# Five edits around the last weights and the stores of an attention and soft-MoE kernel

## The chip, the core and the metric

The kernel runs on one core of a Trainium2 chip. The metric is device time in microseconds (us) of one execution. Five engines work from queues of their own: TensorE (PE in the profile; PEld is its weight load), VectorE (DVE), ScalarE (ACT), GpSimd (POOL) and SyncE (SP). Data moves between the chip's DRAM and the on-chip memory by 16 DMA engines, which the profile shows as a mean busy share and as GB/s. GB/s counts the bytes that are written, so a load of float32 that is cast to bfloat16 on its way shows half of what it reads.

## The reference, cut to what matters

```
scores = q @ k^T / 8, masked                 # q, k, v: (4, 8, 768, 64) float32
a = softmax(scores);  attn = a @ v           # heads 0, 2, 6 causal; the others: 4 first keys + window of 64
x = attn as (3072, 512)
logits = x @ phi                             # phi: (512, 32)
slot_input = softmax(logits, over the 3072 rows)^T @ x       # (32, 512), 4 slots for each of 8 experts
slot_out[e] = relu(slot_input[e] @ w1[e]) @ w2[e]            # w1: (8, 512, 1024), w2: (8, 1024, 512)
out = softmax(logits, over the 32 slots) @ slot_out          # (3072, 512) float32
```

q, k and v are 6.3 MB each, w1 and w2 16.8 MB each, phi 64 KB, and the output is 6.3 MB.

## The kernel before

The program writes down every piece of work as an operation with its engines, an estimated duration, a key, the operations it depends on and the buffers it takes. A small list scheduler in the kernel (`Plan.run`) then places them in order of time, and the instructions are emitted in that order; each engine runs its own list strictly in order. So the keys and estimates decide the order, and the chip's time is what comes of it.

**Loads.** All of q, k, v and the weights but half of w1[0] are loaded by GpSimd (`dma`, L343 to L351), one queue, in a fixed order, cast to bfloat16 on the way. The order ends with the w2 matrices; the last two, 14 and 15 in the code's count (experts 6 and 7 of w2), are loaded in column halves of 256 (`load_half`, L395): left half of 14, left half of 15, right half of 14, right half of 15 (L976 to L979). SP issues three loads at the start (`sp_front`, L480): half of w1[0], the flags, and phi, in this order. phi is cast by DVE (L548), transposed twice by PE and copied to its place (L534 to L555); later products of x and phi read it.

**Attention** runs batch by batch, two heads at a time: scores on PE (L665), exponentials on ACT (L735), masks on DVE (L681), products with v on PE (L809), normalisation on DVE (L833), transposes, and the sums for the slots.

**The experts** follow once all rows are there: products with w1 (L1017), relu (L1027), transposes, and products with w2 (`w2_op`, L1050 to L1066), which add all experts into one bank. Experts 0 to 5 are done for all 512 columns, then experts 6 and 7 for the left 256 columns, and later for the right 256. While PE waits for the last weight of a half, `wait_zeros` (L1070) has it multiply zeros: three such products of 448 columns before the last product of the left half (ZT0), two before that of the right half (ZT1).

**The output.** The sums of a half are scaled into `slot_out` by one instruction (`emit_so`, L1110 to L1115; the scheduler gives both to ACT). Then each block of 128 rows takes one product on PE (L1130) and one scaled copy from the bank on DVE (L1140) or ACT (L1138) into a staging buffer. The first 12 blocks, three groups of four, are done in column halves: all left halves once the left half of `slot_out` is there, all right halves once the right half is there. The other 12 blocks are done for all 512 columns at the end. A group of four blocks is 512 rows of the output, and partition p holds rows 4p to 4p+3.

**The stores** (`store`, L1146). Left halves of group 0: two stores by GpSimd, of one and of three blocks. Left halves of groups 1 and 2: two stores each by SP, of two blocks. Right halves: two stores for each group by SP. The last three groups: one store of 1 MB each by SP.

Of the kernel before, what the change touches and what calls it, by code (L numbers as in the profile page):

```python
# [14 lines left out]
ACT = mybir.ActivationFunctionType  # L15
# [211 lines left out]
def kernel(  # L227
# [13 lines left out]
    nc = tc.nc  # L241
# [5 lines left out]
    NE, DM, F = moe_w1.shape  # L247
# [6 lines left out]
    banks = []  # L254
# [20 lines left out]
    phf = sb.tile([P, 4 * NS], F32, name="phf")  # L275
# [33 lines left out]
    def tr_bf(s, n):  # L309
# [6 lines left out]
    slot_out = mk[:, 640:1152]  # L316
# [4 lines left out]
    pl = Plan({"S8": 11, "QT": 2, "KT": 2, "VT": 1, "VB": 2, "VF": 3, "PT": 2, "PTX": 2, "XB": 2,  # L321
               "XT": 1, "SC": 2, "TR": 2, "PV": 1, "BK": 8})
# [6 lines left out]
    def on(eng, occ, late=0.18):  # L329
        return {eng: (occ, occ + late)}  # L330
# [12 lines left out]
    def dma(name, nbytes, buf, dst, src, deps=()):  # L343
        if len(chain) >= 8:
            deps = list(deps) + [chain[-8]]
        iss = pl.op("issue " + name, on("POOL", 0.645, 1.4), -100, deps=list(deps) + [fifo[0]],
                    acq=[buf] if buf else [], lead=1.3, emit=lambda o: nc.gpsimd.dma_start(dst(), src))  # L347
        fifo[0] = iss
        took = nbytes / (395000.0 if nbytes == 1 << 20 and name != "w0" else 423000.0)
        chain.append(pl.op("land " + name, {"DMA": (took, took + 1.85 + 0.05 * len(chain))}, -100, deps=[iss] + chain[-1:], lead=5.2))  # L350
        return chain[-1]  # L351

# [23 lines left out]
    NW, NSPLIT = 2 * NE, 2  # L376
    wbuf = [Buf("S8") for _ in range(NW)]
    wland = [None] * NW
# [11 lines left out]
    def w_half(i, c):  # L390
        return late_mem[i]()[:, 2048 * c:2048 * (c + 1)].rearrange("p (a f) -> p a f", a=8)

    hland = {}

    def load_half(i, c, deps=()):  # L395
        src = moe_w2[i - NE].rearrange("(fi fo) d -> fi fo d", fo=8)[:, :, 256 * c:256 * (c + 1)]
        hland[i, c] = dma(f"w{i}.{c}", 1 << 20, None, lambda: w_half(i, c), src, deps=deps)

    def load_w(i, deps=()):
        if i == 0:  # L400
# [79 lines left out]
    def sp_front(o):  # L480
        nc.sync.dma_start(w0f, moe_w1[0].rearrange("(di h x) f -> h di (x f)", h=2, x=2)[0])
        nc.sync.dma_start(ri, ri_src)
        nc.sync.dma_start(phf, moe_phi.rearrange("(p a) s -> p (a s)", a=4))

    load_part("q", 0, 0)
    load_part("k", 0, 0)
# [202 lines left out]
    for b in range(B):  # L689
        for n in range(4):  # L690
            p = 4 * b + n
# [55 lines left out]
        for ns in ([(0, 1), (2, 3)] if b == 0 else [(0, 1, 2, 3)]):  # L747
# [18 lines left out]
            def emit_mx(o, b=b, ns=ns):  # L766
# [5 lines left out]
                      emit=emit_mx)  # L772
# [274 lines left out]
    so = Buf("BK")  # L1047
    w2o = {}

    def w2_op(e, c0, c1):  # L1050
        def emit_w2(o):
            e4, g0 = e // 4, e % 4
            for fo in range(8):
                g = fo % 4
                nc.tensor.matmul(banks[so.slot][32 * g:32 * (g + 1), 256 * c0:256 * c1],
                                 hT_t[e4][:, fo, 32 * g0:32 * (g0 + 1)], w_row(NE + e, fo) if c1 - c0 == 2 else w_half(NE + e, c0)[:, fo, :],
                                 start=(e == 0 and fo < 4), stop=(e == NE - 1 and fo >= 4),
                                 tile_position=(0, 32 * g), skip_group_check=True)

        land = [wland[NE + e]] if c1 - c0 == 2 else [hland[NE + e, c0]]  # L1060
        o = pl.op(f"W2.{e}" + ("" if c1 - c0 == 2 else f".{c0}"), on("PE", 0.22 * (c1 - c0), 0.27),
                  kt + (29 + e if c0 == 1 else 16 + e),
                  deps=[hte[e // 4]] + land + [w2o[c] for c in range(c0, c1) if c in w2o],
                  acq=[so] if e == 0 else [], emit=emit_w2, mode="c32", mm=8)
        for c in range(c0, c1):
            w2o[c] = o  # L1066

# [2 lines left out]
    def wait_zeros(name, n, key, dep, first=False):  # L1070
        def emit_z(o):
            for _ in range(n):
                nc.tensor.matmul(banks[zw.slot][:, 0:448], ident, zt, start=True, stop=True)

        pl.op(name, pe(190, n), key, deps=[dep], acq=[zw] if first else [], rel=[zw], emit=emit_z, mode="full", mm=n)
# [3 lines left out]
    whole = w2o[0]  # L1079
    for c in range(2):  # L1080
        for e in range(NE - NSPLIT, NE):
            w2_op(e, c, c + 1)
            if e == NE - 2:
                wait_zeros(f"ZT{c}", 2 if c else 3, kt + (29.5 + e if c else 22.5), w2o[c], c == 0)

    def out_lhs(gi, r):
        return expT[:, r, 128 * gi:128 * (gi + 1)]
# [19 lines left out]
            o_rw[gi] = a  # L1107
    so_e = []
    for c in range(2):
        def emit_so(o, c=c):  # L1110
            d_, s_ = slot_out[:, 256 * c:256 * (c + 1)], banks[so.slot][:, 256 * c:256 * (c + 1)]
            if o.eng == "ACT":
                nc.scalar.activation(d_, s_, ACT.Copy, scale=rcs[:, 0:1])
# [11 lines left out]
    def out_tile(m, gi, r, c0, c1, key):  # L1125
        bf, w = Buf("BK"), 256 * (c1 - c0)
        cs = slice(256 * c0, 256 * c1)

        def emit_om(o):
            nc.tensor.matmul(banks[bf.slot][:, 0:w], out_lhs(gi, r), slot_out[:, cs], start=True, stop=True)  # L1130

        a = pl.op(f"OM.{gi}.{r}.{c0}", on("PE", 0.06 + w / 2400.0, 0.27), key, deps=so_e[c0:c1], acq=[bf],
                  emit=emit_om, mode="full", mm=1)

        def emit_oe(o):
            d, sc_ = ot_view(gi)[:, r, cs], rrow[:, 4 * gi + r:4 * gi + r + 1]
            if o.eng == "ACT":
                nc.scalar.activation(d, banks[bf.slot][:, 0:w], ACT.Copy, scale=sc_)  # L1138
            else:
                nc.vector.tensor_scalar(d, banks[bf.slot][:, 0:w], sc_, None, op0=ALU.mult)  # L1140

        x, y = (0.24 + w / 1070.0, 0.13 + w / 960.0)
        oe[m, gi, r] = pl.op(f"OE.{gi}.{r}.{c0}", {"ACT": (x, x + 0.19), "DVE": (y, y + 0.17)}, key, deps=[a, o_rw[gi]],
                             rel=[bf], emit=emit_oe)

    def store(eng, m, gi, r0, r1, cs, key):  # L1146
        def emit_st(o):
            dst = out[512 * gi:512 * (gi + 1), :].rearrange("(p r) d -> p r d", r=4)
            (nc.gpsimd if eng == "POOL" else nc.sync).dma_start(dst[:, r0:r1, cs], ot_view(gi)[:, r0:r1, cs])

        pl.op(f"ST.{m}.{gi}.{r0}", on(eng, 0.7), key, deps=[oe[m, gi, r] for r in range(r0, r1)], emit=emit_st)
# [70 lines left out]
```

## Time and profile before

| what | us |
|---|---|
| median of 3 runs | 147.88 (147.87 to 148.34) |
| the profiled execution, its own time | 147.56 |
| span from its first to its last instruction | 145.8 |
| time outside the span, 147.56 less 145.8 | 1.76 |
| first left product of the output on PE, start | 125.69 |
| first right product of the output on PE, start | 130.44 |
| last issue of a store by SP, end | 137.97 |

The page of the profile gives busy time by engine, the span in 40 slices, the DMA queues, and the chain of work that ended last. Queue q0 ("software_dynamic") carries what GpSimd issues, q1 ("hardware_dynamic") what SP issues. A DMA share over 1 means that the packets of one engine overlap. Times inside the span count from its start.

### The profile page before, as it was taken

The numbers are of one execution on the slowest core, as the hardware profiler recorded it, in microseconds if no ns is written. First come the engines' busy times: TensorE is split into PE (matmuls) and PEld (weight loads), VectorE is DVE, ScalarE is ACT, GpSimd is POOL, SyncE is SP. The second block draws the span as 40 slices with busy tenths as digits, with TensorE's granted clock in tenths as the row PEclk, the third lists the DMA queues.
The fourth block names the chain that finished last, engine by engine and source line by source line (L and its number), as shares of the span: only waits on it lengthen the run. The fifth ranks groups of instructions, "written<-read, shape, count | busy, mean of one in ns | idle before, by whom it ended". The sixth has DMA issues, their size and how long they took to land.

```text
span 145.8 us, 4941 instructions
## 1 busy us (share of the span) xinstructions
PE 124.6 (85%) x2134; PEld 82.3 (56%) x2134; DVE 110.8 (76%) x254; ACT 107.9 (74%) x147; POOL 40.5 (28%) x73
## 2 busy tenths in 40 slices
PE   6959989999999999999989999999959899869100
PEld 4437566676776758776548766666737355444000
DVE  1796399999999999999799899999983312449700
ACT  3152799999999988999998999999971461549300
POOL 6988631310311470100170011405380000110000
PEclk9985699999999999999999999999995999999965
DMA  5999999999999999999999999999999999999995
GB/s 135 277 208 211 215 215 214 212 216 214 215 214 214 216 215 214 216 214 211 215 214 215 214 216 219 212 217 215 217 210 215 211 194 197 185 321 362 407 420 247
DMA packets 14648, 33.40 MB, mean 229 GB/s; under 512 B 867, under 2 KB 7651, under 8 KB 14115
## 3 DMA queue, kind: packets, MB, share of 16 engines
q0 software_dynamic: 11184, 26.22, 92.9%
q1 hardware_dynamic: 3442, 6.88, 12.7%
q8 instruction: 16, 0.26, 0.6%
q14 instruction: 6, 0.04, 0.1%
HBM read 52.49 MB, written 6.29 MB: 403 GB/s over the span
## 4 chain that ended last, share of the span: by engine, by line
PE 28%; DVE 25%; DMA 18%; ACT 15%; issue 6%; POOL 1%; SPq 0%; DVEq 0%; ACTq 0%; POOLq 0%
DMA qk<-in_moe_w_dram 15%; ACT pt L735 11%; PE sc L665 6%; DVE pt L681 5%; PE pv L809 5%; DVE xv L833 5%; DMA phf<-in_moe_phi_dram 4%; DVE qk L336 3%; PE tr L613 3%; PE tr L639 3%; PE bk L1130 3%; PE tr L872 2%; DVE slot L1140 2%; DVE vf L714 2%; PE tr L845 2%
## 5 line engine op out<-in xcount | busy, mean ns | idle before, releaser
L735 ACT ACTIVATE pt<-sc 128x1024 bf16<-128x1024 f32 x80 | 77.0, 1049 | 3.0 <-PE sc L665 2.8
L665 PE MATMUL sc<-qk 64*128 64x512 bf16 (+3 forms) x256 | 31.3, 311 | 1.2 <-ACT pt L735 0.8
L681 DVE TENSOR_TENSOR pt<-pt,msk 128x1024 bf16<-128x1024 bf16 (+1 forms) x48 | 29.0, 609 | 2.0 <-ACT pt L735 1.8
L809 PEld LDWEIGHTS <-pt 128*128 128x128 bf16 x640 | 23.7, 98 | 6.2 <-issue 5.2
L809 PE MATMUL pv<-vx,pt 128*128 128x65 bf16 x320 | 25.9, 194 | 0.3 <-DVE xv L833 0.2
L809 PE MATMUL pv<-vf,pt 128*128 128x65 bf16 x320 | 21.6, 196 | 0.9 <-DVE xv L833 0.9
L347 POOL DMA_DIRECT2D slot<-in_moe_w_dram x11 | 7.8, 705 | 39.3 <-PE tr L639 29.5
L639 PE MATMUL tr<-ident,slot 128*64 128x128 bf16 (+1 forms) x448 | 16.3, 219 | 0.4 <-ACT qk L334 0.3
L336 DVE COPY qk<-tr 128x768 bf16<-128x768 bf16 (+2 forms) x33 | 15.1, 481 | 1.5 <-PE tr L613 1.3
L639 PEld LDWEIGHTS <-slot 128*64 128x64 bf16 (+1 forms) x448 | 13.1, 109 | 5.1 <-issue 4.8
L833 DVE TENSOR_TENSOR xv<-pv,rs 128x768 bf16<-128x768 f32 (+1 forms) x17 | 15.5, 910 | 0.6
L665 PEld LDWEIGHTS <-qk 64*128 64x128 bf16 x256 | 10.4, 94 | 9.6 <-issue 3.3
L1140 DVE TENSOR_SCALAR slot<-bk,rrow 128x256 f32<-128x256 f32 (+1 forms) x19 | 9.2, 561 | 2.2 <-PE bk L1130 2.2
L896 POOL COPY expT<-eT 128x192 bf16<-128x192 bf16 x12 | 7.4, 657 | 12.2 <-ACT eT L879 12.2
L336 DVE COPY xv<-tr 128x512 bf16<-128x512 bf16 (+2 forms) x20 | 7.9, 409 | 2.4 <-PE tr L613 2.2
L845 PE MATMUL tr<-ident,xv 128*128 128x128 bf16 x96 | 8.4, 224 | 1.3 <-DVE xv L833 0.9
L613 PE MATMUL tr<-ident_u,slot 96*64 96x96 bf16 x192 | 7.3, 238 | 1.9 <-DVE phi L553 1.4
L613 PEld LDWEIGHTS <-slot 96*64 96x64 bf16 x192 | 6.3, 133 | 4.5 <-issue 4.1
L336 DVE COPY xT<-tr 128x768 bf16<-128x768 bf16 (+1 forms) x14 | 7.5, 538 | 1.1 <-PE tr L845 1.1
L1138 ACT ACTIVATE slot<-bk,rrow 128x256 f32<-128x256 f32 (+1 forms) x17 | 7.7, 569 | 0.9 <-PE bk L1130 0.9
L699 PE MATMUL tr<-ident,xv 128*128 128x128 bf16 x96 | 8.1, 220 | 0.0
L845 PEld LDWEIGHTS <-xv 128*128 128x128 bf16 x96 | 6.0, 99 | 2.9 <-DVE xv L833 1.7
(123 smaller groups left out, 169.0 us busy)
## 6 DMA issues: line engine op xcount, KB each, us to landing
slot<-in_moe_w_dram POOLq DMA_DIRECT2D x10, 1024.0 KB, 24.5
out_dram<-slot SPq DMA_DIRECT2D x3, 1024.0 KB, 6.2
out_dram<-slot SPq DMA_DIRECT2D x10, 256.0 KB, 3.2
slot<-in_q_dram POOLq DMA_DIRECT2D x2, 768.0 KB, 19.4
slot<-in_k_dram POOLq DMA_DIRECT2D x2, 768.0 KB, 24.1
qk<-in_moe_w_dram SPq DMA_DIRECT2D x1, 1024.0 KB, 6.1
slot<-in_v_dram POOLq DMA_DIRECT2D x2, 512.0 KB, 21.3
qk<-in_moe_w_dram POOLq DMA_DIRECT2D x1, 1024.0 KB, 17.5
```

Of the source, the lines that this page charges most:

```text
L336: nc.vector.tensor_copy(dst, src)
L347: acq=[buf] if buf else [], lead=1.3, emit=lambda o: nc.gpsimd.dma_start(dst(), src))
L613: nc.tensor.transpose(t[64 * i:64 * (i + 1), :, :, s, :], rv[:, i, 8 * c + s, :], ident_u)
L639: nc.tensor.transpose(t[64 * i:64 * (i + 1), :, s, :], rv[:, i, 8 * c + s, :], ident[0:R, 0:R])
L665: nc.tensor.matmul(scb[sc.slot][:, i, c:c + 128 * nb], kk, qq.rearrange("p b c -> p (b c)"), start=True, stop=True)
L681: nc.vector.tensor_tensor(pT, pT, mh, op=ALU.mult)
L699: nc.tensor.transpose(t[:, 128 * j:128 * (j + 1)], vT[:, 6 * n + j, :], ident)
L735: nc.scalar.activation(pTs[PTb[b, n].slot][:, :, 512 * g:512 * (g + 1)], scb[sc.slot], ACT.Exp, scale=scale)
L809: nc.tensor.matmul(pvb[:, bk, c:c + 65], lt, rhs, start=(j == 0), stop=(j == i))
L833: nc.vector.tensor_tensor(xo, pvw[:, :, :, 0:64], r.rearrange("p i (j o) -> p i j o", o=1).to_broadcast([P, 2, i1 - i0, 64]), op=ALU.mult)
L845: nc.tensor.transpose(t[:, 128 * i:128 * (i + 1)], xv[:, i, 128 * n:128 * (n + 1)], ident)
L1140: nc.vector.tensor_scalar(d, banks[bf.slot][:, 0:w], sc_, None, op0=ALU.mult)
```

## The change

1. **No zeros in the left wait.** ZT0, the three products with zeros between the left product of expert 6 and that of expert 7, is gone. The other zeros stay as two products, but now stand in the middle of expert 7's right half.
2. **Scaling on two engines.** Each half of `slot_out` is scaled by two instructions: ACT takes 96 columns, DVE 160. The output's products wait for both.
3. **The last weight's halves in two loads each.** Each column half of weight 15 is loaded as two DMAs of four of its eight rows for each partition, and its eight matmuls are split into four and four, each four waiting for its own load.
4. **All left stores by GpSimd.** Groups 1 and 2 become one store of four blocks each, issued by GpSimd behind the two of group 0. SP no longer issues left stores.
5. **phi in five pieces**, of 32, 32, 32, 16 and 16 partitions, each a DMA by SP.

The planner's estimate of a load's rate (L349) is changed with it, so that it still takes the halves for the slower ones.

```diff
-        took = nbytes / (395000.0 if nbytes == 1 << 20 and name != "w0" else 423000.0)
+        took = nbytes / (395000.0 if "." in name and name[0] == "w" else 423000.0)
...
     def load_half(i, c, deps=()):
         src = moe_w2[i - NE].rearrange("(fi fo) d -> fi fo d", fo=8)[:, :, 256 * c:256 * (c + 1)]
-        hland[i, c] = dma(f"w{i}.{c}", 1 << 20, None, lambda: w_half(i, c), src, deps=deps)
+        n = 2 if i == NW - 1 else 1
+        hland[i, c] = [dma(f"w{i}.{c}.{x}", (1 << 20) // n, None, lambda x=x: w_half(i, c)[:, 8 * x // n:8 * (x + 1) // n, :],
+                           src[:, 8 * x // n:8 * (x + 1) // n, :], deps=() if x else deps) for x in range(n)]
...
-        nc.sync.dma_start(phf, moe_phi.rearrange("(p a) s -> p (a s)", a=4))
+        for p0, p1 in ((0, 32), (32, 64), (64, 96), (96, 112), (112, 128)):
+            nc.sync.dma_start(phf[p0:p1], moe_phi.rearrange("(p a) s -> p (a s)", a=4)[p0:p1])
...
-    def w2_op(e, c0, c1):
+    def w2_op(e, c0, c1, x=0, n=1):
+        fos = range(8 * x // n, 8 * (x + 1) // n)
...
         for e in range(NE - NSPLIT, NE):
-            w2_op(e, c, c + 1)
-            if e == NE - 2:
-                wait_zeros(f"ZT{c}", 2 if c else 3, kt + (29.5 + e if c else 22.5), w2o[c], c == 0)
+            for x in range(len(hland[NE + e, c])):
+                w2_op(e, c, c + 1, x, len(hland[NE + e, c]))
+            if e == NE - 2 and c:
+                wait_zeros("ZT", 2, kt + 29.5 + e, w2o[c], True)
...
-        so_e.append(pl.op(f"SO.{c}", {"ACT": (0.37, 0.55), "DVE": (0.37, 0.55)}, kt + 25 if c == 0 else kt + 37, deps=[w2o[c], o_rc], rel=[so],
-                          emit=emit_so))
+        x = 256 * c
+        so_e.append([pl.op(f"SO.{c}.{eng}", {eng: (0.25, 0.4)}, kt + 25 if c == 0 else kt + 37, deps=[w2o[c], o_rc], rel=[so],
+                           emit=lambda o, x0=x0, x1=x1: emit_so(o, x0, x1))
+                     for eng, x0, x1 in (("ACT", x, x + 96), ("DVE", x + 96, x + 256))])
...
-    for gi, r0, r1 in [(0, 0, 1), (0, 1, 4)] + [(gi, x, x + 2) for gi, n in halved[1:] for x in (0, 2)]:
-        store("SP" if gi else "POOL", "l", gi, r0, r1, slice(0, 256), kt + 31 + gi + 0.1 * r0)
+    for gi, r0, r1 in [(0, 0, 1), (0, 1, 4)] + [(gi, 0, n) for gi, n in halved[1:]]:
+        store("POOL", "l", gi, r0, r1, slice(0, 256), kt + 31 + gi + 0.1 * r0)
```

Up to the last products with w2, the order of instructions on PE, DVE and ACT is unchanged by it, and on SP and GpSimd only the split loads differ.

More of the change, by code (lines that the diff above doesn't have):

```diff
@@ L1048 @@
     w2o = {}
-    def w2_op(e, c0, c1):
+    def w2_op(e, c0, c1, x=0, n=1):
+        fos = range(8 * x // n, 8 * (x + 1) // n)
         def emit_w2(o):
             e4, g0 = e // 4, e % 4
-            for fo in range(8):
+            for fo in fos:
                 g = fo % 4
@@ L1058, in emit_w2 @@
                                  tile_position=(0, 32 * g), skip_group_check=True)
-        land = [wland[NE + e]] if c1 - c0 == 2 else [hland[NE + e, c0]]
-        o = pl.op(f"W2.{e}" + ("" if c1 - c0 == 2 else f".{c0}"), on("PE", 0.22 * (c1 - c0), 0.27),
-                  kt + (29 + e if c0 == 1 else 16 + e),
+        land = [wland[NE + e]] if c1 - c0 == 2 else [hland[NE + e, c0][x]]
+        o = pl.op(f"W2.{e}" + ("" if c1 - c0 == 2 else f".{c0}") + (f".{x}" if x else ""), on("PE", 0.22 * (c1 - c0) / n, 0.27),
+                  kt + (29 + e if c0 == 1 else 16 + e) + 0.1 * x,
                   deps=[hte[e // 4]] + land + [w2o[c] for c in range(c0, c1) if c in w2o],
-                  acq=[so] if e == 0 else [], emit=emit_w2, mode="c32", mm=8)
+                  acq=[so] if e == 0 else [], emit=emit_w2, mode="c32", mm=len(fos))
         for c in range(c0, c1):
@@ L1109, with emit_so @@
     for c in range(2):
-        def emit_so(o, c=c):
-            d_, s_ = slot_out[:, 256 * c:256 * (c + 1)], banks[so.slot][:, 256 * c:256 * (c + 1)]
+        def emit_so(o, x0, x1):
+            d_, s_ = slot_out[:, x0:x1], banks[so.slot][:, x0:x1]
             if o.eng == "ACT":
@@ L1130, in emit_om @@
             nc.tensor.matmul(banks[bf.slot][:, 0:w], out_lhs(gi, r), slot_out[:, cs], start=True, stop=True)
-        a = pl.op(f"OM.{gi}.{r}.{c0}", on("PE", 0.06 + w / 2400.0, 0.27), key, deps=so_e[c0:c1], acq=[bf],
+        a = pl.op(f"OM.{gi}.{r}.{c0}", on("PE", 0.06 + w / 2400.0, 0.27), key, deps=sum(so_e[c0:c1], []), acq=[bf],
                   emit=emit_om, mode="full", mm=1)
```

## The prediction

> **What bounds the kernel now.** I read the page's DMA rows first, then the busy windows at the two ends, then the chain of waits with the timeline around it.
>
> ```profile
> GB/s 135 277 208 211 215 215 214 212 216 214 215 214 214 216 215 214 216 214 211 215 214 215 214 216 219 212 217 215 217 210 215 211 194 197 185 321 362 407 420 247
> ...
> HBM read 52.49 MB, written 6.29 MB: 403 GB/s over the span
> ```
>
> From the third slice (7 us) to the thirty-second (116 us) the loads write 207 to 219 GB/s, twice that read, with no hole; then 185 to 197 up to 127 us, where the half weights come. Reads and writes together keep the memory at 403 GB/s over the whole span. So the transfers are the bound, and what attention does on the engines beside them is covered. What is left to see is how the DMA passes from loading to storing.
>
> ```profile
> 124.00:125.00 1.00, 1.00 (x16) 0.33 (x11) 0.05 (x1) 0.00 (x0) 0.00 (x0) 1.00 1.47 207
> 126.00:127.00 1.00, 0.96 (x8) 0.56 (x7) 1.00 (x3) 0.89 (x3) 0.22 (x1) 1.00 1.34 186
> 127.00:128.00 1.00, 0.99 (x13) 0.38 (x13) 1.00 (x4) 1.00 (x4) 0.90 (x2) 1.00 0.96 147
> 128.00:129.00 1.00, 0.52 (x6) 0.17 (x3) 0.44 (x2) 0.40 (x2) 0.22 (x1) 1.00 1.15 294
> 129.00:130.00 1.00, 0.54 (x16) 0.32 (x16) 0.00 (x0) 0.09 (x1) 0.00 (x0) 1.00 0.99 358
> 130.00:131.00 1.00, 0.81 (x16) 0.69 (x14) 0.49 (x2) 0.53 (x2) 0.00 (x0) 1.00 1.00 367
> 143.00:144.00 1.00, 0.00 (x0) 0.00 (x0) 0.00 (x0) 0.00 (x0) 0.00 (x0) 0.50 1.01 426
> 144.00:145.00 1.00, 0.00 (x0) 0.00 (x0) 0.00 (x0) 0.00 (x0) 0.00 (x0) 0.50 0.20 82
> ```
>
> The last three columns are the clock, the DMA share and GB/s. Loading the half weights shows a share of 1.47. It falls to 1.34 and then 0.96 in the two microseconds before 128, though the last load has not landed: some DMA engines have finished their part and have nothing to do. From 129 on the share is 1.0 without a gap until 144.2. The end is that of the stores.
>
> ```profile
> 108.08 21.34 DMA qk<-in_moe_w_dram
> 129.42 0.04 issue
> 129.46 0.43 PE bk L1055 x8
> 129.91 0.48 ACT msk L1113
> 130.39 0.04 issue
> 130.44 1.62 PE bk L1130 x12
> ...
> 136.22 1.32 DVE slot L1140 x2
> ```
>
> The chain goes through the landing of the last half weight (129.42), eight matmuls, the scaling and the right products. But it ends at 137.54, and the DMA writes on for 6.7 us. The copies run ahead of the stores, so an earlier right half helps the end only if the DMA would otherwise stand still.
>
> **The change part by part.** The sum is made against the profiled execution: 147.56 us, its span of 145.8 and 1.76 outside. It ran 0.32 under the median of the runs shown, 147.88.
>
> *Left wait and scaling (edits 1, 2, and 3 for the left half).*
>
> ```profile
> 123.71 0.40 PE L1055 MATMUL bk<-pt,xT 128*32 128x256 bf16 x8
> 124.04 0.74 PE L1073 MATMUL bk<-zt,ident 128*128 128x448 bf16 x3
> 124.71 0.40 PE L1055 MATMUL bk<-qk,xT 128*32 128x256 bf16 x8
> 125.17 0.47 ACT L1113 ACTIVATE msk<-bk,rcs 128x256 bf16<-128x256 f32 x1 [4.38 <-PE bk L1055]
> 125.69 2.01 PE L1130 MATMUL bk<-msk,expT 128*128 128x256 bf16 x12 [0.58 <-ACT msk L1113]
> 126.78 1.44 POOL L1149 DMA_DIRECT2D out_dram<-slot  x2 [17.83 <-DVE slot L1140]
> ```
>
> The last left product starts at 124.71 behind the zeros, not behind a load. Its weight lands two halves ahead of 129.42: 1.05 MB written at 196 GB/s (the row for 116 to 126 below) take 5.4 us, so at an estimated 124.0. PE is free of expert 6 at 124.11. It gains about 0.6.
>
> ```profile
> L1140 DVE TENSOR_SCALAR slot<-bk,rrow 128x256 f32<-128x256 f32 x13 | 5.3, 477 | 2.2 <-PE bk L1130 2.2
> ...
> L1140 DVE TENSOR_SCALAR slot<-bk,rrow 128x512 f32<-128x512 f32 x6 | 4.0, 744 | 0.0
> ```
>
> A scaled copy on DVE costs (744 - 477) / 256 = 1.04 ns a column and 0.21 us besides, so 160 columns take about 0.38 against ACT's 0.47; ACT's 96 are shorter. That is 0.1 for each half. Left products and left stores therefore come about 0.7 earlier: the first store is issued near 126.1. PE waits for two engines now; behind it stand only the output's products, which need both anyway. No clock is at risk: PE's gap is near nothing, since 124.11 and 124.0 meet.
>
> *What the 0.7 is worth.* The slack DMA time before 128 is (1.47 - 1.34) / 1.47 + (1.47 - 0.96) / 1.47 = 0.44 us of the whole DMA. That is the most it can bring. I take **nothing**. The engines that idle there are those that finished loading early; the last ones load until 129.42, and every store has a share for them too. The share of 1.0 after 129 says that from then on all are busy, so the late ones set the end with their whole share of the stores, however early the others started. The Trainium skill, "DMA: Bandwidth & Descriptors", section "Why a DMA increments its semaphore by 16 and not by 1", says that a DMA is split over up to 16 engines which finish independently. The fall of the share from 1.47 to 0.96 while PE still waits until 129.46 agrees; by that rule the 0.44 is not to be had.
>
> *Right half (edits 2, 3 and the moved zeros).* Four matmuls instead of eight follow the last landing (0.43 becomes 0.21), and the scaling is 0.1 shorter: the right products start 0.3 earlier. The two zeros (0.55 us) follow the first quarter, which lands an estimated 0.26 MB / 196 GB/s = 1.3 us before 129.42. They end near 128.9, before the last landing, so they cost nothing; were the quarters only 0.7 apart, some 0.1. On DVE the right scaling stands ahead of a reciprocal and copies with slack. The 0.3 is hidden: at 129.42 over 1.2 MB of left stores remain, over 3 us of DMA work. Without that cover it would count in full.
>
> *The extra loads.* GpSimd issues two more, and each earlier issue took 0.87 to 0.90:
>
> ```profile
> 105.45 0.90 POOL L347 DMA_DIRECT2D pt<-in_moe_w_dram  x1 [2.29 <-PE pv L809]
> ...
> 108.08 0.88 POOL L347 DMA_DIRECT2D qk<-in_moe_w_dram  x1
> ```
>
> Even at two more of 0.9 the queue is done near 111, far ahead of the transfers, and nothing else stands on GpSimd until 126. The number of packets stays; two more completions for each engine I put at 0.05 (between 0 and 0.2, by one packet each).
>
> *All left stores by GpSimd.* 1.05 MB move from q1 to q0. The rows for 116 to 126, 129.5 to 131 and 131.2 to 137 (packets, MB, share of 16 engines) are:
>
> ```profile
> q0 software_dynamic: 3485, 1.96, 139.1%
> ```
>
> ```profile
> q0 software_dynamic: 95, 0.33, 57.0%
> q1 hardware_dynamic: 235, 0.23, 43.9%
> ```
>
> ```profile
> q1 hardware_dynamic: 2185, 2.19, 108.2%
> ```
>
> SP's half-row stores go out in packets of about 1 KB, at 2.19 MB / 5.8 us = 378 GB/s when alone. GpSimd's go out in packets of about 3.5 KB: 0.33 MB in 57.0% of 1.5 us, so 386 GB/s at a share of 1, and 386 x 1.08 = 417 if they overlap as SP's do. Beside each other the two make (0.33 + 0.23) / 1.5 = 373. For 1.05 MB that is 2.78 us at 378, 2.52 at 417, 2.72 at 386, 2.81 at 373: between 0.26 gained and 0.04 lost. I take **0.2 gained**, near the upper end, since the left stores will mostly be alone. SP's four issues leave its queue; GpSimd gains two. At 0.72 each (1.44 for two), four take until about 129, while the late DMA engines load.
>
> The left stores also no longer share engines with the last load. From 128 to 129.4 q1 moved 0.20 MB:
>
> ```profile
> q0 software_dynamic: 200, 0.22, 66.3%
> q1 hardware_dynamic: 203, 0.20, 40.9%
> ```
>
> If all of that had pushed the load back, it would land 0.20 MB / 294 GB/s = 0.7 earlier; if q1 used only engines that were done, nothing. I take nothing, since engines had been idle for a microsecond before; and behind the loads on q0 the stores lose what they got done early, which is the same 0.2 MB.
>
> *phi in five pieces.*
>
> ```profile
> 1.55 0.34 SPq L483 DMA_DIRECT2D phf<-in_moe_phi_dram  x1
> ...
> 7.14 0.40 DVE L548 CAST phi<-phf 128x128 bf16<-128x128 f32 x1 [0.23 <-DMA phf<-in_moe_phi_dram]
> ```
>
> Four more issues of 0.34 keep SP until 3.3 instead of 1.9, with nothing behind them for 120 us. The bytes queue behind the 1 MB load of SP in any case. DVE waited 0.23 for phi. So the start moves between 0.23 earlier and, if every issue counted, 1.4 later. I take zero. Even 1.4 later, PE would come to the left product of expert 6 at 125.1 instead of 123.71, and its twelve left products (2.0 us) and expert 6's right one would be done by 129, still ahead of 129.42; the loads run ahead of attention without a hole and do not follow it.
>
> **Sum:** -0.2 (stores on q0) + 0.05 (completions) = -0.15. 147.56 becomes 147.4 for such an execution, and 147.88 becomes **147.7** for a median.
>
> **Rivals.**
>
> *The gap is filled (faster).* If early engines take work off the late ones, or the late ones finish sooner without SP's packets, the 0.44 counts as well: 147.88 - 0.15 - 0.44 = 147.3. With the 0.7 of the landing instead it would be 147.0. For it speaks the falling share before 128; against it the steady 1.0 after 129.
>
> *The new stores are not gathered (slower).* A left store of a whole group is a new shape: 512 rows of 1 KB. If GpSimd's queue sends them as single rows, they go as its small loads do: 1.96 MB in 139.1% of 10 us is 141 GB/s at a share of 1 for packets of 562 bytes. With 1 KB packets at the same time each, that is 257. Then 1.05 MB take 4.08 us instead of 2.78: 1.3 more on every engine, and 147.88 + 0.05 + 1.3 = 149.2. It decides below about 330 GB/s, where 1.05 MB take 3.2 us, 0.4 more. Against it speaks the row of 95 packets, 3.5 KB each, for stores of the same rows. The Trainium skill, same page, section "SWDGE vs HWDGE vs iDMA", gives 4096 bytes as the preferred packet on GpSimd's path; those 95 packets agree.
>
> *It does not do what it says.* If the left weight lands near 124.7, removing zeros brings nothing. The left half gains 0.1 instead of 0.7, and the time is still 147.7: this is part of the forecast.
>
> **How the numbers follow.** About 0.3%, 0.44 us, is what a measurement of this kernel can tell from no change. Forecast, transfers bound and only the packets matter: 0.60, from 147.45 to 148.0. Gap filled: 0.28, at 147.0 to 147.4. Slower, by ungathered stores: 0.12, at 148.3 to 149.2. The line between same and faster is at 147.44, where the forecast's lower end meets the second case. So faster 0.28, same 0.60, slower 0.12. The range takes in the forecast, the gap filled, and the loose runs of before (up to 148.34): 147.0 to 148.3.
>
> **What would show it.** Right: q1 moves nothing before the right stores; q0's packets after 128 stay near 3.5 KB; the first left product starts near 125.0 and the first right one near 130.1; the last share of 1.0 still ends at 144.0 to 144.2. The forecast is wrong if that end moves by more than 0.4, if the share dips under 0.95 after 129.5, or if the last landing leaves 129.4 by more than 0.3. If phi's cast starts after 7.6 and the first left product with it, edit 5 was mis-sized.

## The result, and the profile after

| what | before | after |
|---|---|---|
| median, us (15 runs each) | 147.65 (147.17 to 148.34) | 149.17 (147.71 to 150.09) |
| ratio after to before | | 1.0093, 95% interval 1.0074 to 1.0113 |
| profiled execution, us | 147.56 | 147.71 |
| first left product of the output, in it | 125.69 | 125.44 |
| first right product of the output, in it | 130.44 | 130.73 |

The change made the kernel 1.5 us slower. The ratio compares means and leaves out the slowest execution of the changed kernel (150.09), so it is a little under 149.17 / 147.65. The forecast, 147.7 in a range from 147.0 to 148.3, is wrong, and the one slower case that it named (ungathered stores) is not what happened.

The profile on record is the fastest of the 15 executions; the other 14 took 148.47 to 150.09. A second execution of the same kernel, run as e3 below (149.72), stands for those. Both are read here side by side.

The page of the profile after looks much like that of before:

```profile
PEclk9985799999999999999999999999999999999955
...
GB/s 144 267 210 212 214 214 216 212 217 211 217 213 213 213 214 213 216 214 213 212 217 216 216 212 213 216 214 216 213 213 214 211 196 197 183 324 351 403 422 252
...
HBM read 52.49 MB, written 6.29 MB: 403 GB/s over the span
```

The loads run without a hole, as before, and the mean over this execution's span is the same 403 GB/s (397 over the longer span of e3). The busy windows at the end (the last three columns are clock, DMA share, GB/s) of this execution:

```profile
127.00:128.00 1.00, 0.66 (x10) 0.22 (x9) 1.00 (x4) 1.00 (x4) 0.90 (x3) 1.00 0.97 170
128.00:129.00 1.00, 0.77 (x6) 0.28 (x6) 0.19 (x1) 0.15 (x1) 0.98 (x2) 1.00 0.97 220
129.00:130.00 1.00, 0.44 (x13) 0.33 (x13) 0.00 (x0) 0.09 (x1) 0.47 (x1) 1.00 0.96 343
130.00:131.00 1.00, 0.52 (x14) 0.43 (x11) 0.52 (x2) 0.26 (x1) 0.00 (x0) 1.00 1.00 410
...
144.00:145.00 1.00, 0.00 (x0) 0.00 (x0) 0.00 (x0) 0.00 (x0) 0.00 (x0) 0.50 0.38 156
```

and the same windows of e3, the usual execution:

```profile
127.00:128.00 1.00, 0.55 (x6) 0.49 (x6) 0.62 (x2) 0.13 (x1) 0.00 (x0) 1.00 0.72 102
128.00:129.00 1.00, 0.99 (x8) 0.57 (x6) 1.00 (x4) 1.00 (x4) 0.46 (x1) 1.00 0.63 79
129.00:130.00 1.00, 0.99 (x16) 0.34 (x14) 1.00 (x4) 1.00 (x4) 0.90 (x3) 1.00 0.34 124
130.00:131.00 1.00, 0.88 (x18) 0.49 (x17) 0.28 (x2) 0.51 (x2) 0.98 (x2) 1.00 0.52 184
...
146.00:147.00 1.00, 0.00 (x0) 0.00 (x0) 0.00 (x0) 0.00 (x0) 0.00 (x0) 0.50 0.36 148
```

Here is the lost time. From 127 to 131 before wrote 147 + 294 + 358 + 367 = 1166 KB, e3 only 102 + 79 + 124 + 184 = 489. At the 378 GB/s of stores the missing 677 KB take 1.8 us, and the span is 147.9 instead of 145.8. DMA engines that have finished their loads have no stores yet. The left stores are late because the left products are, as the rows of PE and GpSimd in e3 show:

```profile
127.45 1.90 PE L1138 MATMUL bk<-msk,expT 128*128 128x256 bf16 x12 [0.86 <-DVE msk L1121]
```

```profile
128.54 2.95 POOL L1157 DMA_DIRECT2D out_dram<-slot  x4 [15.22 <-DVE slot L1148]
```

Before, these were at 125.69 and 126.78. The 1.8 us of delay go back to the start of the execution. SP's queue, then DVE, of the profile after:

```profile
1.52 2.60 SPq L486 DMA_DIRECT2D phf<-in_moe_phi_dram  x5
```

```profile
9.19 0.23 DVE L551 CAST phi<-phf 128x128 bf16<-128x128 f32 x1 [2.18 <-DMA phf<-in_moe_phi_dram]
```

and in e3:

```profile
9.16 0.23 DVE L551 CAST phi<-phf 128x128 bf16<-128x128 f32 x1 [1.71 <-DMA phf<-in_moe_phi_dram]
```

phi's cast starts 2.0 us later than before (7.14), and DVE stands still for it. The first exponentials on ACT start at 17.41 in the profile after and at 18.24 in e3, against 15.94 before. Then the two executions part. In the profile after the granted clock is 0.50 from about 9.6 to 16.4, for 6.8 us as before; in e3 from 10.8 to 21.0, for 10.2 us. The sums for the slots come at 115.05 in the one (before: 114.97) and at 117.22 in the other. So the execution on record was lucky: it had a shorter stretch at half clock than e3, and none at 109 where before had one. That these hid the late phi is likely but not shown. In e8 below the cast is at 9.02 and the stretch is 6.8 us too, but it lies from 15.3 to 22.1, and the sums come at 117.06. The last row of waits to read is that of the scaling, in the profile after:

```profile
124.03 0.55 PE L1060 MATMUL bk<-qk,xT 128*32 128x256 bf16 x8
124.63 0.34 ACT L1119 ACTIVATE msk<-bk,rcs 128x96 bf16<-128x96 f32 x1 [3.75 <-PE bk L1060]
125.00 0.38 DVE L1121 TENSOR_SCALAR msk<-bk,rcs 128x160 bf16<-128x160 f32 x1 [0.86 <-ACT msk L1119]
125.44 1.90 PE L1138 MATMUL bk<-msk,expT 128*128 128x256 bf16 x12 [0.86 <-DVE msk L1121]
...
129.57 0.29 PE L1060 MATMUL bk<-qk,xT 128*32 128x256 bf16 x4 [0.56 <-DMA qk<-in_moe_w_dram]
129.91 0.34 ACT L1119 ACTIVATE msk<-bk,rcs 128x96 bf16<-128x96 f32 x1 [1.76 <-PE bk L1060]
130.29 0.38 DVE L1121 TENSOR_SCALAR msk<-bk,rcs 128x160 bf16<-128x160 f32 x1 [2.10 <-ACT msk L1119]
130.73 1.03 PE L1138 MATMUL bk<-msk,expT 128*128 128x256 bf16 x8 [0.48 <-DVE msk L1121]
```

The last left product does start 0.7 earlier, at 124.03. But DVE's scaling waits for ACT's: what DVE waited for is not PE but the other half of the same scaling. The two take 0.34 + 0.38 one after the other, where one instruction took 0.47.

### The profile page after: what moved, and what is told of

Read it like the earlier page. It is cut to its first block, busy times and chain, and to the rows that moved or that the text cites. A ratio compares the mean times of both kernels' runs of the same rounds, so it can differ in the third digit from the quotient of the medians.

```text
span 145.9 us, 4944 instructions
## 1 busy us (share of the span) xinstructions
PE 122.7 (84%) x2131; PEld 81.5 (56%) x2131; DVE 112.4 (77%) x256; ACT 107.4 (74%) x147; POOL 43.2 (30%) x77
## 3 DMA queue, kind: packets, MB, share of 16 engines
q1 hardware_dynamic: 2418, 5.83, 10.8%
## 4 chain that ended last, share of the span: by engine, by line
DVE 26%; PE 25%; DMA 17%; ACT 16%; issue 5%; POOL 2%; SPq 2%; DVEq 0%; ACTq 0%; POOLq 0%
DMA qk<-in_moe_w_dram 13%; ACT pt L738 12%; PE sc L668 5%; DVE pt L684 5%; PE pv L812 5%; DVE xv L836 5%; DMA phf<-in_moe_phi_dram 4%; DVE qk L336 3%; PE tr L642 3%; PE bk L1138 3%; PE tr L616 2%; PE tr L875 2%; DVE slot L1148 2%; DVE vf L717 2%; PE tr L848 2%
## 5 line engine op out<-in xcount | busy, mean ns | idle before, releaser
L812 PE MATMUL pv<-vf,pt 128*128 128x65 bf16 x320 | 21.1, 194 | 0.9 <-DVE xv L836 0.9
L1138 PE MATMUL bk<-msk,expT 128*128 128x256 bf16 (+1 forms) x36 | 6.7, 307 | 1.5 <-DVE msk L1121 1.3
```

Of the source, the lines that this page charges most:

```text
L812: nc.tensor.matmul(pvb[:, bk, c:c + 65], lt, rhs, start=(j == 0), stop=(j == i))
```

## The experiments

My theory after the result: phi in pieces lands late, attention follows it, and the left stores are then too late for DMA engines that run out of loads. Rivals were the moved zeros, the two-engine scaling, the stores by GpSimd, and, for phi itself, the five transfers as such. All ratios are to before on the same chip, with their 95% intervals; "before" there had medians of 147.69 to 147.85.

### One edit undone, and the change again

**e1**, the changed kernel with phi in one piece:

```diff
-        for p0, p1 in ((0, 32), (32, 64), (64, 96), (96, 112), (112, 128)):
-            nc.sync.dma_start(phf[p0:p1], moe_phi.rearrange("(p a) s -> p (a s)", a=4)[p0:p1])
+        nc.sync.dma_start(phf, moe_phi.rearrange("(p a) s -> p (a s)", a=4))
```

> The changed kernel with phi in one piece again, all else as changed. Theory P (phi's five pieces reach DVE 2 us later, and in most executions that late start goes through attention to the output): the 1.4 to 1.5 us of slowdown are gone, so 147.4 to 147.8 and level with before, or up to 0.4 under it by the other four edits. Theory S (the left stores on GpSimd's queue, or the split last load, cost the time in most executions): stays near 149.2.

148.52, ratio 1.0037 (1.0006 to 1.0068). The cast is at 7.37, the first left product at 125.08. phi is the larger part of the loss, but something is left: this is over the 147.4 to 147.8 that I expected.

**e2**, before with phi in five pieces and nothing else (that part of the change's diff alone):

> The kernel before with phi in five pieces alone. Theory P: slower by about 1.5, near 149.2, with DVE's cast of phi near 9.2 instead of 7.1. Theory S: level with before, 147.65.

149.89, ratio 1.0136 (1.0096 to 1.0176): this edit alone costs 2.0 us, at least as much as the whole change (e3 below, with an overlapping interval). Its rows on DVE and PE:

```profile
10.09 0.23 DVE L549 CAST phi<-phf 128x128 bf16<-128x128 f32 x1 [3.19 <-DMA phf<-in_moe_phi_dram]
10.23 0.15 DVE L445 TENSOR_SCALAR xT<-ri 1x16 f32<-1x16 int32 x1
```

```profile
10.38 0.61 PE L538 MATMUL tr<-ident,phi 128*32 128x128 bf16 x4 [3.83 <-DVE phi L549]
```

```profile
127.74 2.01 PE L1131 MATMUL bk<-msk,expT 128*128 128x256 bf16 x12 [0.58 <-ACT msk L1114]
```

The view of phi's tile in e2 (durations and times from issue to landing as minimum, median and maximum):

```profile
L484 SPq DMA_DIRECT2D phf<-in_moe_phi_dram x5: 319/421/1027, 1.5 to 3.9; - x5
...
DMA to landing us min/median/max: 5.8/6.2/6.8
```

and in before:

```profile
L483 SPq DMA_DIRECT2D phf<-in_moe_phi_dram x1: 339/339/339, 1.5 to 1.5; - x1
...
DMA to landing us min/median/max: 5.6/5.6/5.6
```

A piece takes no less time to land than the whole, a little more in fact, and the last one is issued at 3.9 instead of 1.5. It is not only the products with phi that then wait. Each engine takes its list in order, and behind phi's cast on DVE stand the flags (L445, at 7.46 before) and the masks made from them, behind phi's transposes on PE those of the first queries and keys (8.85 before, 11.99 here). So the first exponentials start at 19.27 instead of 15.94. The left products are 2.05 later than before, and the execution (149.77) is 2.2 longer. In e3, the whole change, the left products come 0.29 before those of e2; the zeros that are gone may be why it loses less, but the intervals do not tell the two apart.

**e3**, the changed kernel again:

> The changed kernel once more, for a profile of an execution like most of its own: the one on record took 147.71 where 14 others took 148.5 to 150.1. Theory P: a profile of about 149 shows the cast of phi near 9.2, the experts' products reached some 1.5 to 2 us later than in the profile of 147.71, and the right stores later by as much. Theory S: the experts' products come as early as in the profile of 147.71, and the time is lost after 125 us. A third reading, that only the granted clock differs: a stretch at half clock lies late in the span, and the start is the same in both.

149.50, ratio 1.0078 (1.0039 to 1.0117). The loss is there in a second series of runs.

**e4**, the changed kernel with phi in two pieces:

```diff
-        for p0, p1 in ((0, 32), (32, 64), (64, 96), (96, 112), (112, 128)):
+        for p0, p1 in ((0, 64), (64, 128)):
```

> The changed kernel with phi in two pieces instead of five. Theory P with a cost for each piece (five pieces came 1.9 us later than one, so 0.5 for each piece beyond the first): the cast near 7.6, and a time 0.3 to 0.5 over that with one piece. Theory S: near 149.2.

149.07, ratio 1.0084 (1.0046 to 1.0122), with the cast at 8.66 and the first left product at 126.91. Two pieces already cost most of it: their issues begin at 1.5 and 2.1, but they take 6.2 to 6.5 to land. The delay is not in proportion to the number of pieces, as I had expected it to be.

### What is left with phi whole

**e5** is e1 with each half scaled by ACT alone, **e6** is e1 with the left stores as before, **e7** is e1 with three zeros in the left wait again and two before the first quarter of the right half.

```diff
# e5
-                     for eng, x0, x1 in (("ACT", x, x + 96), ("DVE", x + 96, x + 256))])
+                     for eng, x0, x1 in (("ACT", x, x + 256),)])
# e6
-    for gi, r0, r1 in [(0, 0, 1), (0, 1, 4)] + [(gi, 0, n) for gi, n in halved[1:]]:
-        store("POOL", "l", gi, r0, r1, slice(0, 256), kt + 31 + gi + 0.1 * r0)
+    for gi, r0, r1 in [(0, 0, 1), (0, 1, 4)] + [(gi, x, x + 2) for gi, n in halved[1:] for x in (0, 2)]:
+        store("SP" if gi else "POOL", "l", gi, r0, r1, slice(0, 256), kt + 31 + gi + 0.1 * r0)
# e7
-            if e == NE - 2 and c:
-                wait_zeros("ZT", 2, kt + 29.5 + e, w2o[c], True)
+            if e == NE - 2:
+                wait_zeros(f"ZT{c}", 2 if c else 3, kt + (29.5 + e if c else 22.5), w2o[c], c == 0)
```

> The changed kernel with phi whole and each half of slot_out scaled by ACT alone again. In the profile after, DVE's part starts only when ACT's is done (0.34 and 0.38 us in a row), so two engines cost 0.3 us a half instead of saving 0.1. Theory A (that serial scaling is what the other four edits lose, against the kernel with phi whole at 148.5): 148.1 to 148.3, and the right products start 0.3 earlier after the last matmul. Rival B (the loss lies in the stores by GpSimd) or C (in the missing zeros): stays at 148.5.

> The changed kernel with phi whole and the left stores as before: groups 1 and 2 by SP in two stores each. Theory B (GpSimd issues one store after the other at 0.74 us each and its queue starts late, so the DMA is short of work between 128 and 130): 147.8 to 148.1, 0.4 to 0.7 under phi whole. Rivals A and C: 148.5. My forecast on record had this the other way: 0.2 slower than phi whole.

> The changed kernel with phi whole and the three products with zeros back in the left wait (and two in the right one, in the place of before). Theory C (without zeros PE is idle enough for its clock to be halved near 126.7, as in the profile with phi whole, and the right half is done at half clock): no half clock between 125 and 135 in the profile, and 147.8 to 148.2. Rivals A and B: 148.5, or 148.6 as the left half comes 0.1 to 0.6 later.

e5: 147.87, ratio 1.0007 (0.998 to 1.0033). e6: 147.80, 1.0005 (0.9979 to 1.003). e7: 148.58, 1.0037 (1.0006 to 1.0068), the same as e1. Putting the zeros back brings nothing back. My reason to try it was the clock: in e1's profile PE waits for the weight before its left products, and the granted clock is 0.50 from 126.4 to 133.3. But e7's is still 0.50 from 130.9 to 134.3, so e7 does not tell what a full clock would be worth there; e6's profiled execution, with 0.50 from 124.0 to 134.3, took 147.97 and shows no large price for it. With either the scaling or the stores undone the median is near that of before, but the intervals of e5 and e6 overlap with that of e1: that each undoes the loss is suggested, not shown.

**e9**, **e10** and **e11** put edits on before one at a time: the two loads and the zeros (edits 1 and 3), the scaling (edit 2), the stores (edit 4). Their diffs are those parts of the change.

> Before, with only two of the five edits: the last weight's halves in two loads each, and the left wait's zeros moved (phi whole, scaling by ScalarE alone, left stores by SP for groups 1 and 2). My theory: left products 0.6 us earlier and right ones 0.3 earlier are both off the path that sets the end, so 147.5 to 147.9, ratio to before 0.997 to 1.001. Rival (the 0.44 us of idle DMA before 128 can be filled by earlier left stores): 147.2 to 147.4, ratio 0.995 to 0.997, faster. The first left product should start near 124.9, before any experiment with late phi.

> Before, with the scaling of each half on two engines alone. My theory: the second scaling waits for the first (0.34 + 0.38 us in the changed kernel's profile against 0.47 to 0.48 for one), so both first products start 0.3 us later: left near 126.0, right near 130.75. The stores that SP issues follow 0.3 later; by the share of time that DMA engines idle before 128 that costs at most 0.3, so 147.7 to 148.1, ratio 1.000 to 1.003. Rival (the price shows only together with stores by GpSimd, whose first bytes come later): ratio 1.000. Rival (it is all of what is left of the loss with phi whole): ratio 1.004, 148.4.

> Before, with all left stores by GpSimd alone. My theory: q0 carries no store bytes in between while GpSimd prepares the next store (0.74 us each, first bytes some 1.2 us after the issue), so DMA engines starve more around 128 to 131; but packets of 4 KB take back some 0.2. Together 147.7 to 148.2, ratio 1.000 to 1.003. Rival (the forecast: 0.2 gained): 147.5, ratio 0.998. Rival (it is all of what is left of the loss with phi whole): ratio 1.004, 148.4.

e9: 147.71, ratio 0.9996 (0.9971 to 1.0021), with the first left product at 125.12. That product came 0.6 earlier and the time is the same: the earlier left half did not fill the 0.44 of idle DMA before 128, which would have been a ratio of 0.997. e10: 147.60, 0.9999 (0.9972 to 1.0027). e11: 148.14, 1.0019 (0.9995 to 1.0043). Alone, the scaling costs nothing that can be measured: its first left product is at 125.57, no later than before, its first right one at 130.89, 0.45 later. Its row on DVE in e10 shows the same order of two as in the changed kernel:

```profile
130.45 0.39 DVE L1115 TENSOR_SCALAR msk<-bk,rcs 128x160 bf16<-128x160 f32 x1 [2.13 <-ACT msk L1113]
```

The stores by GpSimd are not faster: the forecast's 0.2 gained would be a ratio of 0.9986, which lies outside the interval; a loss of up to 0.6 us lies in it. Whether the two edits cost more together than one by one stays open: 1.0037 for both and 1.0019 and 0.9999 for each have overlapping intervals.

### Why the late phi costs

**e8**, e2 with 30 more products of zeros on PE while it waits for phi, so that its clock falls less:

```diff
-        fill(10)
+        fill(40)
```

> The kernel before with phi in five pieces and 30 more products with zeros on PE while it waits for phi (they feed nothing). With phi in five pieces PE stood idle for 3.8 us and its clock was then halved for 10.2 us instead of 6.8. Theory P1 (the longer half clock makes most of the loss): the half clock is 6.8 or less again and the time falls from 149.9 to 148.5 or less. Theory P2 (the late data alone make it): the time stays at 149.5 to 150, whatever the clock.

150.83, ratio 1.0185 (1.0119 to 1.0252), above both theories. The half clock at the start did shrink to 6.8 us, but the sums for the slots came at 117.06, as late as in e2 (117.00). The run is no clean test of the clock, since the stretch moved to 15.3 to 22.1, where attention begins. A better one is the profile of e9: with phi whole it has 10.2 us at half clock too, from 7.7 to 18.0, and yet its sums come at 114.19 and its time is 147.72. So a long stretch at half clock is not enough to make the loss. The end of e8 is later still than its left products (127.79) would make it. Its DMA queues in the stretch from 131 to 134:

```profile
q1 hardware_dynamic: 635, 0.60, 58.3%
q0 software_dynamic: 109, 0.39, 37.4%
q8 instruction: 1, 0.02, 3.4%
```

One load of instructions took 3.4% of 16 engines for 3 us, that is 1.6 us of one engine's time, and after 147 only three packets of the stores were left. That the one made the other late is a guess from one execution.

**e13** and **e14**: before with phi whole and every transfer as it was, but DVE repeats one copy of the mask's distances ahead of the cast, four and eight times in all (the same output):

```diff
# e14; e13 has range(4)
-        nc.vector.tensor_copy(edist[:, 256:768].rearrange("p (a c) -> p a c", a=2),
-                              edist[:, 0:256].rearrange("p (o c) -> p o c", o=1).to_broadcast([P, 2, 256]))
+        for _ in range(8):
+            nc.vector.tensor_copy(edist[:, 256:768].rearrange("p (a c) -> p a c", a=2),
+                                  edist[:, 0:256].rearrange("p (o c) -> p o c", o=1).to_broadcast([P, 2, 256]))
```

> Before with phi whole; VectorE repeats one copy of the mask's distances three times ahead of phi's cast (same output), so that the cast starts some 1 us later (near 8.1), with the transfers as before. My theory (what counts is when attention starts, not the number of transfers): half of the delay or so is free, as the profiled execution of the changed kernel with sums for the slots at 115.05 was; 147.8 to 148.7, ratio 1.001 to 1.007. Rival (the five transfers themselves cost): 147.7, ratio 1.000.

> Before with phi whole; VectorE repeats the same copy seven times ahead of phi's cast, so that the cast starts 2 to 2.5 us later (9.2 to 9.6), with the transfers as before. My theory: as with phi in five pieces alone, sums for the slots after 116.5, the first left product of the output after 127, a DMA share under 0.6 in one of the microseconds from 127 to 131, and 149.0 to 150.0, ratio 1.008 to 1.016. Rival (the five transfers themselves cost): 147.7, ratio 1.000, with the DMA share at 0.95 or more from 128 on.

e13: 148.28, ratio 1.0024 (0.9999 to 1.0049). e14: 150.37, ratio 1.0153 (1.0117 to 1.0189), a little over my range. In e14, DVE, PE and the busy windows:

```profile
6.62 3.34 DVE L442 COPY edist<-edist 128x512 bf16<-128x512 bf16 x8
9.87 0.22 DVE L549 CAST phi<-phf 128x128 bf16<-128x128 f32 x1
```

```profile
128.78 2.00 PE L1131 MATMUL bk<-msk,expT 128*128 128x256 bf16 x12 [0.58 <-ACT msk L1114]
```

```profile
127.00:128.00 1.00, 1.00 (x19) 0.33 (x11) 0.13 (x1) 0.00 (x0) 0.00 (x0) 1.00 0.86 125
128.00:129.00 1.00, 0.42 (x11) 0.29 (x4) 0.00 (x0) 0.47 (x1) 0.00 (x0) 1.00 0.47 63
129.00:130.00 1.00, 0.97 (x8) 0.57 (x6) 0.92 (x3) 0.81 (x3) 0.14 (x1) 1.00 0.03 8
130.00:131.00 1.00, 0.98 (x12) 0.41 (x11) 1.00 (x3) 1.00 (x5) 0.90 (x2) 1.00 0.00 0
131.00:132.00 1.00, 1.00 (x20) 0.38 (x16) 0.52 (x2) 0.51 (x3) 0.30 (x1) 1.00 0.99 344
```

Without one more transfer, a cast at 9.87 costs what five pieces cost. For two microseconds the DMA does next to nothing: the loads are over and the first left store is not yet written. This settles it for the late start against the transfers as such. The 1166 - 196 = 970 KB not written from 127 to 131 take 2.6 us at 378 GB/s, and this execution (150.56) is 3.0 longer than that of before.

**e12** is before with phi whole and issued ahead of SP's other two loads, **e15** the same with five pieces.

```diff
 # e12; in e15 the five pieces stand in this place
+        nc.sync.dma_start(phf, moe_phi.rearrange("(p a) s -> p (a s)", a=4))
         nc.sync.dma_start(w0f, moe_w1[0].rearrange("(di h x) f -> h di (x f)", h=2, x=2)[0])
         nc.sync.dma_start(ri, ri_src)
-        nc.sync.dma_start(phf, moe_phi.rearrange("(p a) s -> p (a s)", a=4))
```

> Before, with phi in one piece issued first on SP, ahead of the half of w1[0] and the flags. My theory (attention late costs, attention early is worth nothing, since the loads run ahead of it and set when the last weight lands): phi's cast between 5.0 and 6.8 instead of 7.14, experts up to 1 us earlier, the time the same: 147.5 to 147.9, ratio 0.997 to 1.001. Rival (the time follows attention both ways): 0.5 us or more faster, 147.0 to 147.3, ratio under 0.997. Rival (w1[0]'s half or the flags, now behind phi, are late for something, or DMA descriptors of phi push q0's first loads): slower, over 148.0.

> Before with phi in five pieces, issued by SP ahead of the half of w1[0] and the flags. My theory: the pieces land by 7.1, the cast starts before 7.6 and the time is that of before with phi whole and first (148.1) or up to 0.3 above, since SP's big load is issued 1.9 us later: 147.8 to 148.4, ratio 1.001 to 1.005. Rival (five transfers land one after another wherever they stand): cast after 8.5 and 149.0 to 150.0. Rival (the half of w1[0] is late for its product, first used by the experts): no, it is used after 114.

e12: 148.11, ratio 1.0024 (1.0006 to 1.0041). The cast is at 6.82 and waits for nothing, yet the time is no better, even 0.2% worse. That is what the rival of something being late behind phi had said, but the flags, now last on SP's queue, are used at 7.37 without a wait, and I have no cause for the 0.2%. e15: 151.76, ratio 1.024 (1.0192 to 1.0288), more than any expectation had. Its SP queue and DVE:

```profile
0.74 2.25 SPq L482 DMA_DIRECT2D phf<-in_moe_phi_dram  x5
3.03 0.42 SPq L483 DMA_DIRECT2D qk<-in_moe_w_dram  x1
3.50 0.35 SPq L484 DMA_DIRECT2D ri<-in_is_retrieval_dram  x1
```

```profile
7.45 0.37 DVE L549 CAST phi<-phf 128x128 bf16<-128x128 f32 x1 [0.55 <-DMA phf<-in_moe_phi_dram]
11.17 0.16 DVE L445 TENSOR_SCALAR xT<-ri 1x16 f32<-1x16 int32 x1 [3.35 <-DMA ri<-in_is_retrieval_dram]
```

phi is in time now, and the flags, 64 bytes, are what DVE waits for until 11.17. They are last on SP's queue, behind the 1 MB half of w1[0], which now starts 2.3 us later and runs beside GpSimd's loads. My expectation asked only for the use of w1[0]'s half after 114 and missed what stands behind it. phi's five pieces, ahead of the big load, land in 1.6 to 4.8 (median 1.7). So it is not phi as such that matters but the small load that lands last, and a place behind the big load makes it late: less so in e12, where the flags were issued at 1.64. The Trainium skill, "DMA: Bandwidth & Descriptors", section "Queues, rings and completion order", says that each DMA engine goes round between the queues that have work, a packet at a time, and takes the descriptors of one queue in order. That agrees with the flags, issued at 3.50 and waited for until 11.17, and with the pieces in e2, which take 6.2 to land for a quarter of the bytes and less.

### One curve for all of them

The first left product and the time of the same profiled execution:

| run | first left product | time |
|---|---|---|
| e11 | 124.91 | 147.65 |
| e9 | 125.12 | 147.72 |
| after | 125.44 | 147.71 |
| e10 | 125.57 | 147.72 |
| before | 125.69 | 147.56 |
| e13 | 126.79 | 148.63 |
| e4 | 126.91 | 149.35 |
| e3 | 127.45 | 149.72 |
| e2 | 127.74 | 149.77 |
| e14 | 128.78 | 150.56 |
| e15 | 129.50 | 151.56 |

Up to 125.7 the time is flat; from there each microsecond of delay costs about one. From before to e14 it is 3.0 us of time for 3.09 of delay. e1 (125.08, 147.84), e6 (125.36, 147.97), e7 (125.15, 147.83) and e12 (125.48, 147.96) lie on the flat part within 0.3. Each point is one execution, though, and the medians of e1 and e7 (148.52 and 148.58) are 0.7 above theirs, so the curve does not hold what is left with phi whole. e5's profiled execution (125.90, 148.63) and e8's (127.79, 151.18) lie 0.9 and 1.4 above the curve, and why is not shown: e5's left and right products ran at half clock, but so did e6's, and e8 had the load of instructions.

No version beats both kernels: e10 and e9, the best, cannot be told from before.

## Why the prediction was wrong

**phi in five pieces: the step that failed.** The forecast said that the start moves "between 0.23 earlier and, if every issue counted, 1.4 later", and "I take zero". It moved 2.0 later (9.19), and 2.95 in e2. The bound counted four further issues of 0.34, 1.4 in all, and a landing as quick as that of the whole. In fact SP needed 2.60 for the five issues (in e2 the median is 0.42 and the longest 1.03), 2.26 more than for one, and each piece took 5.8 to 6.8 to land in e2 against 5.6. The "nothing behind them for 120 us" was true of SP; what counted was what stands behind phi on DVE and PE.

**The cover of that step failed as well, and this is the costlier error.** "Even 1.4 later, PE would come to the left product ... still ahead of 129.42; the loads run ahead of attention without a hole and do not follow it." The loads indeed do not follow: in e14 they are over soon after 129 (share 0.03 from 129 to 130), while the last one landed at 129.42 before. But the forecast held the delay against the wrong date. The left half has to be ready not when the last weight lands but when the first DMA engines run out of loads, at 127, or they stand still. The windows that I quoted (1.34, then 0.96) show that date. I used them to show that an earlier left half brings nothing, which e9 confirms, and did not ask what a later one costs. It costs about one for one, since before stood at the bend of the curve.

**Left wait and zeros.** Right: the last left product started at 124.03 (the forecast had 0.6 to 0.7 gained), and this is worth nothing (e9, and e7 against e1). "No clock is at risk" held in the profile after, but not in e1's, whose PE was busy for only 0.40 of the 2.08 us from 123.0 to 125.08 and ran at half clock from 126.4; what that costs is not shown. The 0.05 for the completions of the extra loads is not shown by any run either; it is within e9's interval.

**Scaling on two engines.** Wrong in sign: 0.1 gained for each half was forecast, 0.3 was lost, since DVE waits for ACT. Hence the first right product at 130.73 and not near 130.1, and the first left one at 125.44 and not 125.0. The Trainium skill, "PSUM — Partial Sum Buffer", section "PSUM bank collisions raise a hardware error", says that two engines may not use the same bank and the same 32 partitions at once, reads included, and that the compiler back end adds a dependency between such instructions. The row of DVE released by "ACT msk L1119" agrees, and both scalings read one bank; no run scales from two banks to test it. By e10 it costs nothing that can be measured alone; with the stores by GpSimd it may be part of e1's 0.37%.

**Stores by GpSimd.** The packets are as forecast. The queues of the profile after, from 126 to 130 and from 129.5 to 131:

```profile
q0 software_dynamic: 906, 0.91, 105.4%
```

```profile
q0 software_dynamic: 150, 0.54, 91.7%
```

q1 does not appear in either, and 0.54 MB in 150 packets is 3.6 KB each, at 0.54 / (0.917 x 1.5) = 393 GB/s for a share of 1 (386 forecast). But the 0.2 does not show in the time. The four issues take 2.94 us one after another (126.53 to 129.47), which I had counted as covered by late loads. And the time of e11 alone excludes such a gain. The rival of ungathered stores is out.

**The right half.** Its quarters did save PE time (0.29 after the landing instead of 0.43), and it was hidden, as forecast.

**What was to show it wrong** did: the share fell to 0.34 and 0.52 after 129 in e3, the end moved by 2, and phi's cast started after 7.6.

## What to carry to other kernels

When a passage from loading to storing is bound by the DMA, as here, the first store has a date: the moment at which the first DMA engines run out of loads. In this kernel being earlier than that was worth nothing and being later cost in full, so "earlier brings nothing" must never be turned into "later costs nothing". A small load that something waits for at the start is not free to split: each piece added an issue and, behind the same big load, took as long to land as the whole, so the last piece set the date. Look at what stands behind its first use in the lists of the engines, too. Before work on one PSUM bank is split over two engines, see whether they may read it at the same time.

## What the runs showed of the hardware that I had not expected

- The granted clock comes in stretches at 0.50 whose length is a multiple of about 3.4 us: 6.8 at the start of before and of the profile after, 10.2 in e2 and e3. With phi whole and its cast at 7.2 to 7.4, the sums for the slots came at 112.21 after no such stretch at the start (e5), at 113.0 after one of 3.4 (e6, e11), at 113.8 to 114.1 after 6.8 (e1, e7) and at 114.19 after 10.2 (e9): from 0.1 to 1.1 us for each 3.4. That may be part of why the profiled execution of after was as fast as before. The Trainium skill, "TensorE: Matmul & The Clock Gate", section "What's actually happening", gives free-running windows of 3413 ns; the lengths of 3.4, 6.8 and 10.2 agree.
- The same 64 KB of phi reach DVE at 7.14 in one transfer, at 8.66 in two and at 9.2 to 10.1 in five, while another queue loads.
- Loads of instructions run beside the stores: 16 KB took 1.6 us of one DMA engine's time in e8. Whether that moved e8's end is not shown.
